# Maxout with two up passes on weight differences, and the first product folded into the down projection

## The chip, the cores and the metric

One core of a Trainium2 chip. The metric is the device time of one execution in microseconds (us), the median of several runs. An execution is also recorded by the hardware profiler; its own time is given beside the span from its first to its last instruction.

## The reference

Attention with exponential features over 8 batches and 8 heads, 576 tokens of 64 elements each, and a maxout feed-forward over the 4608 tokens that come out of it:

```
def phi(x):
    proj = np.einsum('bhsd,df->bhsf', x, w_phi)
    proj = proj - np.max(np.abs(proj), axis=-1, keepdims=True)
    return np.concatenate([np.exp(proj), np.exp(-proj)], axis=-1)
q_p, k_p = (phi(q), phi(k))
kv = np.einsum('bhsf,bhsd->bhfd', k_p, v)
z = np.sum(k_p, axis=2)
num = np.einsum('bhsf,bhfd->bhsd', q_p, kv)
den = np.einsum('bhsf,bhf->bhs', q_p, z)[..., None] + 1e-06
x = (num / den), heads side by side: 4608 x 512
h = np.maximum(np.maximum(x @ w1, x @ w2), x @ w3)     # w1, w2, w3: 512 x 768
return h @ w_out                                       # w_out: 768 x 512
```

## The kernel before

Products are in bf16 with fp32 accumulation in eight PSUM banks. The attention runs in 16 units of four heads (two units make a batch); the feed-forward in nine chunks of 512 tokens: chunk b takes the first 512 tokens of batch b and needs units 2b and 2b+1, chunk 8 takes the last 64 tokens of every batch and needs them all.

A unit's steps, with the names of the profile. q and k are loaded in bf16 (`qk_bf`; units 0 to 3 through GpSimd's DMA queue, which casts on the way, unit 0 in halves; their short tails and all later units come in fp32 through SP's queue as `q_raw`, `k_raw` and are cast by an engine). They are transposed (`tps` to `qkT` by TensorE for units 0 to 3, by DMA later), projected (`psq`, `psk`, `psg`), the maxima taken by VectorE (`mqp`, `mk`), the exponentials by ScalarE (`Ek`, and `Eq` from a second product `psm`). v is multiplied by the scale `em` (`vab`, `vtl`), k's features times v give `kvps` and `kv_sb`, q's features times that give `psn`, VectorE divides (`x_sb`), and TensorE or a DMA transposes into `xT` (`pxT`), the tokens that the feed-forward reads.

A chunk before the change: for each of the three weights and each of six blocks of 128 columns of the hidden layer, four products of 512 columns into `ups`. The first weight's result is copied to `hT` (by ScalarE or VectorE), the second and the third are taken in by VectorE with a maximum (three passes, L757, L763, L765). Then for each of four tiles of 128 tokens six products into `ops` (L784), an eviction to `osb` (L795) and a store. Until the first chunk can start, TensorE is kept busy with products that nothing reads (`warm`).

The weights are loaded once, through GpSimd's queue, with q and k of the first units around them in the order of a string (`ORDER`; in it w0 is w1 of the reference, w1 is w2, w2 is w3, and w3 is w_out).

All steps are nodes of a planner, which runs when the kernel is built. It simulates engines and queues with a cost in microseconds for every node, picks at each moment the ready node with the lowest rank (tables `RANKS` by group of units, `LAGS`, `EVAC` for the feed-forward), chooses the engine where there are several, and so fixes the order of instructions on each engine. On the chip every engine goes through its own order, and waits where an operand or a buffer isn't ready.

Of the kernel before, what the change touches and what calls it, by code (L numbers as in the profile page):

```python
# [10 lines left out]
EXP = mybir.ActivationFunctionType.Exp  # L11
ALU = mybir.AluOpType
# [4 lines left out]
DM = H * D  # L17
DFF = 768
# [17 lines left out]
ORDER = "q0 k0 q1 k1 w0 q2 k2 w1 w2 w3 q3 k3"  # L36
# [6 lines left out]
OSB = 4  # L43
LEAD = 99
# [92 lines left out]
]  # L137
LAGS = [7.954, 12, 11.152, 10.425, 9.54, 8.084, 9.876, -8.613, -11.269]
EVAC = -17.068
FFN = {"up": 0, "down": 0, "t1": 1, "t2": 1, "h": 1, "osb": 1, "store": 1}  # L140


def rank(n):

    if n.kind in FFN:
        return 2 * n.u + LAGS[n.u] + n.at / 11.0 + FFN[n.kind] * EVAC
    if n.kind in ("const", "phi"):
        return -99.0
# [12 lines left out]
class Queues:  # L161
# [4 lines left out]
    UNEVEN = 1.5  # L166
# [11 lines left out]
    def issue(self, n, eng, t, cost):  # L178

        pipes, mine = self.pipes, "POOL" if eng == "POOL" else "SP"  # L180
        other = "SP" if mine == "POOL" else "POOL"
        if n.hold is not None:
            cost = max(cost, pipes[mine] + n.hold - t)
            if n.hold > 0:
                cost = max(cost, pipes[other] + n.hold - t)
        done = t + cost
        end = done
        if n.pipe:
            at = max(done, pipes[mine])
            both = max(0.0, pipes[other] - at)  # L190
            end = at + n.pipe
            if both:
                turns = self.packet[other] / n.packet
                pipes[other] += min(n.pipe, both / turns)
                end += min(both, n.pipe * turns)
            pipes[mine] = end
            self.packet[mine] = n.packet
            if both:
                end += self.UNEVEN
        end += n.lat  # L200
        if not n.pipe and max(pipes.values()) > done:
            end += self.BEHIND
        self.ends[mine] += [end] * n.dmas
        return done, end
# [85 lines left out]
def kernel(  # L290
# [146 lines left out]
    def attention(u):  # L437
# [13 lines left out]
        for what in range(3):  # L451
            raw = raw_bufs(u)[what]
            if what < 2 and by_pe:
                for i, (t0, t1) in enumerate(((0, 8), (8, MT)) if u < HALVES else ((0, MT),)):
                    def main(what=what, t0=t0, t1=t1):
# [281 lines left out]
    def chunk(c_i, ready, tokens_of, out_rows, n_out):  # L737
# [11 lines left out]

        before = [None] * JT  # L750
        for i in range(3):
            for j in range(JT):
                ups = bank("ups", [P, SM])

                def up(i=i, j=j, ups=ups):
                    for ct in range(CT):
                        nc.tensor.matmul(ups(), lhsT=w_bf[i][:, ct, j * P:(j + 1) * P], rhs=tokens_of(ct),  # L757
                                         start=(ct == 0), stop=(ct == CT - 1))
                a = ff("up", {"PE": 0.87}, up, ready + [w_nodes[i]], [ups], pe=True)

                def ev(n_, i=i, j=j, ups=ups):
                    if i == 0:
                        copy_on[n_.eng](hT()[:, j, :], ups())  # L763
                    else:
                        nc.vector.tensor_tensor(hT()[:, j, :], hT()[:, j, :], ups(), ALU.max)  # L765
                e = ff(("t1", "t2", "h")[i], {"ACT": 0.5, "DVE": 0.61} if i == 0 else {"DVE": 0.64}, None,
# [3 lines left out]
                if i == 2:  # L770
                    evac.append(e)
        steps.append(pes)
        for tt in range(SM // P):
# [4 lines left out]
            for i in range(halves):  # L778
# [3 lines left out]
                def down(j0, j1, tt=tt, ops_=ops_, cols=cols, width=width):  # L782
                    for j in range(j0, j1):
                        nc.tensor.matmul(ops_()[:, 0:width], lhsT=hT()[:, j, tt * P:(tt + 1) * P], rhs=wout_bf[:, j, cols],  # L784
                                         start=(j == 0), stop=(j == JT - 1))
                if tt == 0:
                    ff("down", {"PE": 0.87}, lambda f=down: f(0, 4), evac[0:4] + [w_nodes[3]], [hT, ops_], pe=True)
                    count[0] -= 1
                j0 = 4 if tt == 0 else 0
                a = ff("down", {"PE": 1.30 / halves * (JT - j0) / JT}, lambda f=down, j0=j0: f(j0, JT), evac + [w_nodes[3]],  # L790
                       [hT, ops_], pe=True)
# [22 lines left out]
    def weights():  # L814
# [4 lines left out]
        for name in ORDER.split():  # L819
            chain += converted[name] if name != "k0" else []  # L820
            if name == "q0" and HALVES:
# [6 lines left out]
    weights()  # L828
    for b in range(B):
        rows = out[b * S:b * S + SM, :].rearrange("(p j) n -> p j n", j=SM // P)  # L830
        chunk(b, units[2 * b]["done"] + units[2 * b + 1]["done"], lambda ct, b=b: xT[:, b, ct, 0:SM],
              lambda tt, rows=rows: [(rows[:, tt, :], slice(0, P))], 1)
    chunk(B, units[UNITS - 1]["done"], lambda ct: xT[:, :, ct, SM:SM + ST],
# [43 lines left out]
```

## Time and profile before

| | |
|---|---|
| median of 3 runs | 322.58 us (322.11 to 323.34) |
| the profiled execution | 323.14 us, span 321.4 us |
| TensorE busy | 303.3 us, 94% |
| VectorE busy | 235.2 us, 73% |
| ScalarE busy | 209.7 us, 65% |
| GpSimd busy | 117.3 us, 36% |
| mean granted TensorE clock | 0.985 |

In the profile TensorE is PE (its loading of stationary operands PEld), VectorE DVE, ScalarE ACT, GpSimd POOL and SyncE SP. A line of a group of instructions gives source line, engine, operation, output and inputs, the count, busy time in us, mean ns of one, and the idle time of the engine before them with what ended it.

### The profile page before, as it was taken

Reading aid. Unit: us, or ns where it says so; the run is one execution under the profiler, and the core shown is the slowest. Engines: PE = TensorE matmul, PEld = TensorE weight load, DVE = VectorE, ACT = ScalarE, POOL = GpSimd, SP = SyncE. Lnnn points to the kernel's source line nnn. Section 1 sums busy time; section 2 is a strip of 40 time slices with the busy share of each in tenths; the row PEclk is TensorE's granted clock in tenths of the full one; section 3 lists DMA queues with packets and bytes.
Section 4 is the critical chain, followed back from the end, with each engine's and each line's share of the span. In section 5 each row is a group of like instructions: output and inputs, shape, how many; then the busy total and the mean of one; then the engine's idle time right before and its main releaser. Section 6 shows DMA issues by size and latency. Waiting matters only on the chain.

```text
span 321.4 us, 7835 instructions
## 1 busy us (share of the span) xinstructions
PE 303.3 (94%) x3088; PEld 170.3 (53%) x3124; DVE 235.2 (73%) x485; ACT 209.7 (65%) x491; POOL 117.3 (36%) x137
## 2 busy tenths in 40 slices
PE   8999599998999999899999999999999999999993
PEld 3466475556555645644645564546545574444442
DVE  4898973975977995988988878976796686081360
ACT  1597885466979897898698796657707961503301
POOL 8633133170486089083561902635006500000000
PEclk9999899999999999899999999999999999999998
DMA  7999999139868797968997599929803013203005
GB/s 121 224 197 228 233 261 242 44 100 228 232 154 203 245 259 156 255 152 157 200 282 196 84 203 253 245 96 194 140 0 134 1 37 81 98 0 112 21 1 131
DMA packets 87882, 49.79 MB, mean 155 GB/s; under 512 B 56101, under 2 KB 83365, under 8 KB 87845
## 3 DMA queue, kind: packets, MB, share of 16 engines
q1 hardware_dynamic: 81140, 43.98, 56.4%
q0 software_dynamic: 6624, 5.24, 10.4%
q8 instruction: 24, 0.39, 0.5%
q10 hardware_dynamic: 80, 0.07, 0.1%
q14 instruction: 14, 0.11, 0.1%
HBM read 34.67 MB, written 9.44 MB: 137 GB/s over the span
## 4 chain that ended last, share of the span: by engine, by line
PE 74%; DVE 11%; issue 5%; ACT 4%; DMA 2%; POOL 2%; DVEq 0%; POOLq 0%
PE ups L757 42%; PE ops L784 12%; PE kvps L677 6%; PE psn L697 4%; DVE mqp L571 3%; ACT Eq L661 3%; PE psq L558 3%; PE psm L649 3%; DVE x_sb L704 3%; DMA qk_bf<-in_k_dram 2%; DVE mk L571 2%; PE warm L424 1%; PE tps L515 1%; ACT Ek L564 1%; DVE osb L795 1%
## 5 line engine op out<-in xcount | busy, mean ns | idle before, releaser
L757 PE MATMUL ups<-xT,w_bf 128*128 128x512 bf16 x620 | 146.3, 379 | 3.2 <-ACT Eq L661 0.8
L765 DVE TENSOR_TENSOR hT<-hT,ups 128x512 bf16<-128x512 bf16 x108 | 72.7, 685 | 38.8 <-PE ups L757 37.9
L757 PEld LDWEIGHTS <-w_bf 128*128 128x128 bf16 x648 | 61.2, 98 | 71.5 <-issue 3.0
L564 ACT ACTIVATE Ek<-psk 128x512 bf16<-128x512 f32 x128 | 69.7, 621 | 25.6 <-PE psk L558 24.2
L661 ACT ACTIVATE Eq<-psm 128x512 bf16<-128x512 f32 (+1 forms) x160 | 75.4, 591 | 12.3 <-PE psm L649 8.7
L614 POOL TENSOR_TENSOR vab<-v_raw,em 128x1024 bf16<-128x1024 f32 (+1 forms) x30 | 54.2, 1821 | 15.8 <-ACT em L609 15.7
L784 PE MATMUL ops<-wout_bf,hT 128*128 128x512 bf16 (+1 forms) x214 | 49.2, 373 | 0.4
L571 DVE TENSOR_REDUCE mqp<-psq 128x4 bf16<-128x512 f32 x64 | 42.9, 683 | 3.8 <-PE psk L558 3.7
L795 ACT COPY osb<-ops 128x512 f32<-128x512 f32 (+1 forms) x25 | 14.5, 578 | 46.4 <-PE ops L784 46.3
L571 DVE TENSOR_REDUCE mk<-psk 128x4 f32<-128x512 f32 x64 | 42.7, 683 | 0.0
L624 POOL CAST vab<-em 128x32 bf16<-128x32 f32 (+1 forms) x12 | 3.8, 316 | 88.8 <-issue 52.6
L763 ACT CAST hT<-ups 128x512 bf16<-128x512 f32 x47 | 27.6, 590 | 10.6 <-PE ups L757 9.9
L704 DVE TENSOR_TENSOR x_sb<-psn,rden 128x320 bf16<-128x320 f32 x64 | 31.5, 492 | 2.2
L784 PEld LDWEIGHTS <-hT 128*128 128x128 bf16 x222 | 20.9, 98 | 22.0 <-DVE hT L765 0.6
L629 POOL TENSOR_TENSOR vtl<-v_raw,em 64x256 bf16<-64x256 f32 x32 | 20.3, 635 | 21.8 <-ACT em L609 20.6
L697 PE MATMUL psn<-kv_sb,Eq 128*128 128x65 bf16 x640 | 24.8, 195 | 2.1 <-DVE mqp L571 1.2
L697 PEld LDWEIGHTS <-Eq 128*128 128x128 bf16 x640 | 23.1, 98 | 5.9 <-issue 1.7
L677 PEld LDWEIGHTS <-Ek 128*128 128x128 bf16 x640 | 23.7, 101 | 4.5 <-ACT vtl L638 1.2
L677 PE MATMUL kvps<-vab,Ek 128*128 128x65 bf16 x512 | 24.3, 198 | 0.3 <-DVE vab L614 0.2
L677 PE MATMUL kvps<-vtl,Ek 128*128 128x65 bf16 x128 | 21.8, 197 | 1.1 <-ACT vtl L638 1.1
L558 PE MATMUL psk<-w,qkT 64*128 64x128 bf16 x256 | 21.0, 217 | 1.2 <-ACT Eq L661 0.8
L558 PEld LDWEIGHTS <-qkT 64*128 64x128 bf16 x512 | 14.6, 94 | 13.4 <-issue 10.6
(61 smaller groups left out, 267.5 us busy)
## 6 DMA issues: line engine op xcount, KB each, us to landing
v_raw<-in_v_dram SPq DMA_DIRECT2D x16, 512.0 KB, 5.8
out_dram<-osb SPq DMA_DIRECT2D x32, 256.0 KB, 2.5
q_raw<-in_q_dram SPq DMA_DIRECT2D x12, 512.0 KB, 5.7
k_raw<-in_k_dram SPq DMA_DIRECT2D x12, 512.0 KB, 6.2
w_bf<-in_moe_w_dram POOLq DMA_DIRECT2D x3, 768.0 KB, 21.5
q_raw<-in_q_dram SPq DMA_DIRECT2D x16, 64.0 KB, 3.8
k_raw<-in_k_dram SPq DMA_DIRECT2D x16, 64.0 KB, 5.9
v_raw<-in_v_dram SPq DMA_DIRECT2D x16, 64.0 KB, 4.4
```

Source lines behind the costliest of these rows:

```text
L558: nc.tensor.matmul(ps[c]()[:, i, :], lhsT=cols[r, :], rhs=w2[r, c, :], start=True, stop=True)
L564: nc.scalar.activation(Ek[s]()[:, t0:t0 + n, :], ps() if n > 2 else ps()[:, :, 1, :], EXP, scale=1.0 - 2.0 * s)
L571: nc.vector.tensor_reduce((mq, mk)[c]()[:, t0:t0 + n], ps() if n > 2 else ps()[:, :, c, :], AXX, ALU.max, apply_absolute_value=True)
L614: (nc.vector if n_.eng == "DVE" else nc.gpsimd).tensor_tensor(vab()[:, g, t0:t1, 0:D], raw_part(u, 2, t0, t1), em()[:, g, t0:t1].unsqueeze ...
L661: nc.scalar.activation(Eqb()[s][:, cols], psm()[:, 0:n * P], EXP, scale=1.0 - 2.0 * s)
L677: nc.tensor.matmul(kvps()[:, ab, g, :], lhsT=Ek[g]()[:, t, :], rhs=vab()[:, g, t, :] if c < 4 else vt()[:, g, pr, ab, :], start=(c == 0), ...
L697: nc.tensor.matmul(psn()[:, c, :], lhsT=Eqb()[g][:, t0:t0 + P], rhs=kv()[:, pr, ab, g, :], start=(g == 0), stop=(g == 1))
L704: nc.vector.tensor_tensor(x_sb()[:, pr, :, ab, :], psn()[:, :, 0:D], rden().to_broadcast([P, 5, D]), ALU.mult)
L757: nc.tensor.matmul(ups(), lhsT=w_bf[i][:, ct, j * P:(j + 1) * P], rhs=tokens_of(ct), start=(ct == 0), stop=(ct == CT - 1))
L763: copy_on[n_.eng](hT()[:, j, :], ups())
L765: nc.vector.tensor_tensor(hT()[:, j, :], hT()[:, j, :], ups(), ALU.max)
L784: nc.tensor.matmul(ops_()[:, 0:width], lhsT=hT()[:, j, tt * P:(tt + 1) * P], rhs=wout_bf[:, j, cols], start=(j == 0), stop=(j == JT - 1))
```

## The change

It rests on max(a, b, c) = a + max(0, b - a, c - a). With a = x w1 the up projection needs products with w2 - w1 and w3 - w1 only, and a's share of the output, x (w1 w_out), is added in the accumulation of the down projection. So:

- VectorE subtracts w1 from w2 and from w3 in place, in bf16, each in two halves of 128 x 1536 (`wd`).
- TensorE transposes w1 (24 transposes, `pwT`), the result is copied to a buffer of `hT`, and multiplied with w_out: four times six products into `pm`. The copies of `pm` (`line_w`) overwrite the first 512 columns of w1.
- A chunk has two up passes. The first is evicted with a maximum with zero, the second with VectorE's maximum as before. Each down tile begins with four products of the tokens with `line_w`, and goes on with the six of `hT` with w_out.
- Eight copies on GpSimd put the last 64 tokens of each batch side by side for the last chunk (into the other columns of w1 and into `x_last`).
- k of unit 0 comes through SP's queue in fp32 (`K0_SP`), with a cast on VectorE or ScalarE.
- The order of loads, `RANKS`, `LAGS`, `EVAC`, the step of the feed-forward's ranks and the planner's rule for two queues at once get other values. So the whole order of instructions is new.

```diff
-ORDER = "q0 k0 q1 k1 w0 q2 k2 w1 w2 w3 q3 k3"
+ORDER = "q0 k0 q1 k1 w0 q2 k2 w3 w1 q3 k3 w2"
...
+K0_SP = 1
...
-LAGS = [7.954, 12, 11.152, 10.425, 9.54, 8.084, 9.876, -8.613, -11.269]
-EVAC = -17.068
-FFN = {"up": 0, "down": 0, "t1": 1, "t2": 1, "h": 1, "osb": 1, "store": 1}
+LAGS = [11.676, 11.801, 9.456, 10.469, 7.828, 8.2, 10.732, 10.134, 2.767]
+EVAC = -53.283
+FFN = {"up": 0, "down": 0, "t1": 1, "h": 1, "osb": 1, "store": 1, "wd": 1, "wt": 0, "we": 1, "wm": 0, "mo": 1}
+STEPS = 8.5
...
-        return 2 * n.u + LAGS[n.u] + n.at / 11.0 + FFN[n.kind] * EVAC
+        return 2 * n.u + LAGS[n.u] + n.at / STEPS + FFN[n.kind] * EVAC
...
-            if both:
+            if both and done > self.CALM:
                 end += self.UNEVEN
...
+    line_w = w_bf[0][:, :, 0:DM]
+    x_last = [w_bf[0][:, :, DM:DFF], const.tile([P, CT, DFF - DM], BF16, name="x_last")]
...
+                    if u == 0 and what == 1 and K0_SP:
+                        def main(t0=t0, t1=t1):
+                            nc.sync.dma_start(raw_part(0, 1, t0, t1).rearrange("p (h j) d -> p h (j d)", j=SM // P),
+                                              k[0, t0 // 4:t1 // 4, 0:SM, :].rearrange("h (p j) d -> p h (j d)", p=P))
...
-        for i in range(3):
+        for i in range(2):
             for j in range(JT):
...
-                        nc.tensor.matmul(ups(), lhsT=w_bf[i][:, ct, j * P:(j + 1) * P], rhs=tokens_of(ct),
+                        nc.tensor.matmul(ups(), lhsT=w_bf[i + 1][:, ct, j * P:(j + 1) * P], rhs=tokens_of(ct),
...
-                a = ff("up", {"PE": 0.87}, up, ready + [w_nodes[i]], [ups], pe=True)
+                a = ff("up", {"PE": 0.87}, up, ready + diffs[i], [ups], pe=True)
...
-                    if i == 0:
-                        copy_on[n_.eng](hT()[:, j, :], ups())
+                    if i == 1:
+                        nc.vector.tensor_tensor(hT()[:, j, :], hT()[:, j, :], ups(), ALU.max)
+                    elif n_.eng == "ACT":
+                        nc.scalar.activation(hT()[:, j, :], ups(), RELU)
                     else:
-                        nc.vector.tensor_tensor(hT()[:, j, :], hT()[:, j, :], ups(), ALU.max)
+                        nc.vector.tensor_scalar_max(hT()[:, j, :], ups(), 0.0)
...
+                def straight(tt=tt, ops_=ops_, cols=cols, width=width):
+                    for ct in range(CT):
+                        nc.tensor.matmul(ops_()[:, 0:width], lhsT=tile_of(ct, tt), rhs=line_w[:, ct, cols],
+                                         start=(ct == 0), stop=False)
...
-                                         start=(j == 0), stop=(j == JT - 1))
-                if tt == 0:
-                    ff("down", {"PE": 0.87}, lambda f=down: f(0, 4), evac[0:4] + [w_nodes[3]], [hT, ops_], pe=True)
...
+                                         start=False, stop=(j == JT - 1))
+                ff("down", {"PE": 0.87 / halves}, straight, ready + lines, [ops_], pe=True)
+                count[0] -= 1
+                a = ff("down", {"PE": 1.30 / halves}, down, evac + [w_nodes[3]], [hT, ops_], pe=True)
...
+    for i in range(2):
+        for h in range(2):
+            def diff(n_, i=i, h=h):
+                dst, c = w_bf[i + 1], slice(2 * h, 2 * h + 2)
+                (nc.vector if n_.eng == "DVE" else nc.gpsimd).tensor_tensor(dst[:, c, :], dst[:, c, :], w_bf[0][:, c, :],
+                                                                           ALU.subtract)
...
+                    nc.tensor.transpose(pwT()[:, i, ct, :], w_bf[0][:, ct, (2 * g + i) * P:(2 * g + i + 1) * P], ident)
...
+                nc.tensor.matmul(pm(), lhsT=w1T()[:, j, ct * P:(ct + 1) * P], rhs=wout_bf[:, j, :],
+                                 start=(j == 0), stop=(j == JT - 1))
+        n_ = wnode("wm", {"PE": 1.30}, mult, turned + diffs[0] + diffs[1] + [w_nodes[3]], [pm, w1T], at=8)
...
+        lasts.append(node("C", 2 * b + 1, {"POOL": 0.4}, lambda b=b: nc.gpsimd.tensor_copy(
+            x_last[b // 4][:, :, b % 4 * ST:(b % 4 + 1) * ST], xT[:, b, :, SM:SM + ST]),
```

More of the change, by code (lines that the diff above doesn't have):

```diff
@@ L11 @@
 EXP = mybir.ActivationFunctionType.Exp
+RELU = mybir.ActivationFunctionType.Relu
 ALU = mybir.AluOpType
@@ L43 @@
 OSB = 4
+K0_SP = 1
+BY_POOL = ()
 LEAD = 99
@@ L165 @@
     BEHIND = 2.5
-    UNEVEN = 1.5
+    UNEVEN, CALM = 1.5, 6.0
     def __init__(self):
@@ L454, in attention, with to_bf16 @@
                 for i, (t0, t1) in enumerate(((0, 8), (8, MT)) if u < HALVES else ((0, MT),)):
+                    if u == 0 and what == 1 and K0_SP:
+                        def main(t0=t0, t1=t1):
+                            nc.sync.dma_start(raw_part(0, 1, t0, t1).rearrange("p (h j) d -> p h (j d)", j=SM // P),
+                                              k[0, t0 // 4:t1 // 4, 0:SM, :].rearrange("h (p j) d -> p h (j d)", p=P))
+                        n_ = nd("L0" if i == 0 else "const", {"SP": 0.62}, main, [], [raw], pipe=0.133 * (t1 - t0), lat=1.7,
+                                at=what, packet=59.0)
+                        def to_bf16(n_, t0=t0, t1=t1):
+                            copy_on[n_.eng](qk()[:, 1, t0:t1, :], raw_part(0, 1, t0, t1))
+                        n_ = nd("C", {"DVE": 0.42, "ACT": 0.55}, None, [n_], [raw, qk])
+                        n_.fn = lambda n_=n_, f=to_bf16: f(n_)
+                        cast[1, i] = cast[1, 1] = n_
+                        continue
                     def main(what=what, t0=t0, t1=t1):
@@ L735, with chunk @@
     last_ff, steps = [None], []
-    def chunk(c_i, ready, tokens_of, out_rows, n_out):
+    def chunk(c_i, ready, tokens_of, tile_of, out_rows, n_out):
         hT = buf("hT", 2, [P, JT, SM], BF16)
@@ L769, in chunk @@
                 before[j] = e
-                if i == 2:
+                if i == 1:
                     evac.append(e)
@@ L780, in chunk, with down @@
                 cols = slice(i * width, (i + 1) * width)
-                def down(j0, j1, tt=tt, ops_=ops_, cols=cols, width=width):
-                    for j in range(j0, j1):
-                        nc.tensor.matmul(ops_()[:, 0:width], lhsT=hT()[:, j, tt * P:(tt + 1) * P], rhs=wout_bf[:, j, cols],
-                                         start=(j == 0), stop=(j == JT - 1))
-                if tt == 0:
-                    ff("down", {"PE": 0.87}, lambda f=down: f(0, 4), evac[0:4] + [w_nodes[3]], [hT, ops_], pe=True)
[L788 to L791, printed above, removed]
+                def straight(tt=tt, ops_=ops_, cols=cols, width=width):
+                    for ct in range(CT):
+                        nc.tensor.matmul(ops_()[:, 0:width], lhsT=tile_of(ct, tt), rhs=line_w[:, ct, cols],
+                                         start=(ct == 0), stop=False)
+                def down(tt=tt, ops_=ops_, cols=cols, width=width):
+                    for j in range(JT):
+                        nc.tensor.matmul(ops_()[:, 0:width], lhsT=hT()[:, j, tt * P:(tt + 1) * P], rhs=wout_bf[:, j, cols],
+                                         start=False, stop=(j == JT - 1))
+                ff("down", {"PE": 0.87 / halves}, straight, ready + lines, [ops_], pe=True)
+                count[0] -= 1
+                a = ff("down", {"PE": 1.30 / halves}, down, evac + [w_nodes[3]], [hT, ops_], pe=True)
                 part = osb or buf("osb", OSB, [P, DM], FP32)
@@ L819, in weights @@
         for name in ORDER.split():
-            chain += converted[name] if name != "k0" else []
-            if name == "q0" and HALVES:
+            if name == "k0" and HALVES:
+                continue
+            chain += converted[name]
+            if name == "q0" and HALVES and not K0_SP:
                 chain[-2:] = [converted["q0"][0], converted["k0"][0], converted["q0"][1], converted["k0"][1]]
@@ L828, with wnode, turn, turned_out @@
     weights()
+    diffs, lines, turned = [[], []], [], []
+    def wnode(*args, at):
+        return node(args[0], 0, *args[1:], at=at)
+    for i in range(2):
[4 more added lines that the diff above has]
+                                                                           ALU.subtract)
+            n_ = wnode("wd", {"DVE": 0.87}, None, [w_nodes[0], w_nodes[i + 1]], [], at=6 * i - 2)
+            n_.fn = lambda n_=n_, f=diff: f(n_)
+            diffs[i].append(n_)
+    w1T = buf("hT", 2, [P, JT, SM], BF16)
+    for g in range(JT // 2):
+        pwT = bank("pwT", [P, 2, CT, P], BF16)
+        def turn(g=g, pwT=pwT):
+            for i in range(2):
+                for ct in range(CT):
+                    nc.tensor.transpose(pwT()[:, i, ct, :], w_bf[0][:, ct, (2 * g + i) * P:(2 * g + i + 1) * P], ident)
+        def turned_out(n_, g=g, pwT=pwT):
+            copy_on[n_.eng](w1T()[:, 2 * g:2 * g + 2, :].rearrange("p i n -> p (i n)"),
+                            pwT().rearrange("p i c n -> p (i c n)"))
+        n_ = wnode("wt", {"PE": 0.6}, turn, [w_nodes[0], n_ident], [pwT], at=4)
+        n_t = node("we", 0, {"ACT": 0.95, "DVE": 1.15}, None, [n_], [pwT, w1T], locks=[pwT], at=4)
+        n_t.fn = lambda n_=n_t, f=turned_out: f(n_)
+        turned.append(n_t)
+    for ct in range(CT):
+        pm = bank("pm", [P, DM])
+        def mult(ct=ct, pm=pm):
+            for j in range(JT):
+                nc.tensor.matmul(pm(), lhsT=w1T()[:, j, ct * P:(ct + 1) * P], rhs=wout_bf[:, j, :],
+                                 start=(j == 0), stop=(j == JT - 1))
+        n_ = wnode("wm", {"PE": 1.30}, mult, turned + diffs[0] + diffs[1] + [w_nodes[3]], [pm, w1T], at=8)
+        n_t = node("mo", 0, {"ACT": 0.5, "DVE": 0.61}, None, [n_], [pm], locks=[pm], at=8)
+        n_t.fn = lambda n_=n_t, ct=ct, pm=pm: copy_on[n_.eng](line_w[:, ct, :], pm())
+        lines.append(n_t)
     for b in range(B):
@@ L831 @@
         chunk(b, units[2 * b]["done"] + units[2 * b + 1]["done"], lambda ct, b=b: xT[:, b, ct, 0:SM],
+              lambda ct, tt, b=b: xT[:, b, ct, tt * P:(tt + 1) * P],
               lambda tt, rows=rows: [(rows[:, tt, :], slice(0, P))], 1)
-    chunk(B, units[UNITS - 1]["done"], lambda ct: xT[:, :, ct, SM:SM + ST],
+    lasts = []
+    for b in range(B):
+        lasts.append(node("C", 2 * b + 1, {"POOL": 0.4}, lambda b=b: nc.gpsimd.tensor_copy(
+            x_last[b // 4][:, :, b % 4 * ST:(b % 4 + 1) * ST], xT[:, b, :, SM:SM + ST]),
+            units[2 * b]["done"] + units[2 * b + 1]["done"] + diffs[0] + diffs[1] + turned, []))
+    chunk(B, lasts, lambda ct: xT[:, :, ct, SM:SM + ST],
+          lambda ct, tt: x_last[tt // 2][:, ct, tt % 2 * P:(tt % 2 + 1) * P],
           lambda tt: [(out[(2 * tt + i) * S + SM:(2 * tt + i + 1) * S, :], slice(i * ST, (i + 1) * ST))
```

2 lines of the change are left out of this document (1 added, 1 removed), and 66 rows, old and new, of the table RANKS.

## The prediction

> **What bounds the kernel now.** I read the page's first part, then busy time by stretch, with the stretches cut at three events: the first up product (46.73), the end of the last attention product (265.30) and the end of the last product of all (316.30).
>
> ```profile
> span 321.4 us, 7835 instructions
> PE 303.3 (94%) x3088; PEld 170.3 (53%) x3124; DVE 235.2 (73%) x485; ACT 209.7 (65%) x491; POOL 117.3 (36%) x137
> ```
>
> ```profile
> core 0: us, PE busy (x) PEld busy (x) DVE busy (x) ACT busy (x) POOL busy (x), PEclk, DMA share, GB/s
> 0.00:46.73 46.73, 41.40 (x567) 26.42 (x568) 38.33 (x92) 32.51 (x81) 22.95 (x39) 0.96 1.12 212
> 46.73:265.30 218.57, 211.19 (x2289) 120.44 (x2319) 175.02 (x359) 163.31 (x388) 94.30 (x98) 0.99 0.70 166
> 265.30:316.30 51.00, 50.74 (x238) 23.47 (x240) 21.41 (x37) 13.87 (x24) 0.00 (x0) 1.00 0.19 57
> 316.30:321.40 5.10, 0.00 (x0) 0.00 (x0) 0.42 (x1) 0.00 (x0) 0.00 (x0) 0.69 0.54 122
> ```
>
> From 46.73 to 316.30, that is 269.57 us, TensorE is the limit: it stands still for 7.38 us in the middle stretch and 0.26 us in the one after, 7.64 in all, while VectorE has 43.6 us free and ScalarE 55.3 in the middle one. Before 46.73 TensorE only looks busy (warm products fill it); there the loads and VectorE set the pace. The last 5.10 us are an eviction and a store, which the change leaves alone.
>
> TensorE's real rates are read from runs of one kind in the chain of waits in order of time (start, length, what), because a single product's duration overlaps the next one.
>
> ```profile
> 4.65 6.64 DMA qk_bf<-in_k_dram
> 11.34 0.63 PE tps L515 x15
> 51.21 1.01 PE tps L515 x32
> 74.51 1.28 PE kvps L677 x40
> 80.06 0.45 PE pxT L718 x5
> 269.57 5.18 PE ops L784 x24
> 295.47 15.54 PE ups L757 x72
> ```
>
> 72 products of 512 columns in 15.54 us and 24 in 5.18 both give 0.216 us each. A transpose takes 0.032 to 0.09 us.
>
> **The change, part by part.**
>
> *TensorE after the first up product.* The three up passes become two: 9 chunks x 6 column blocks x 4 = 216 products go, 216 x 0.216 = -46.6 us. In the down projection each of 36 tiles gets 4 products with w1 w_out, the last of them split into two half-width ones: worth 144, +31.1. Making w1 w_out takes 24 products (`pm`), +5.2. In the built order of instructions, unit 2's 40 kvps products now come behind the first up product (+1.3, the row of 40) and unit 3's 32 tps transposes come ahead of it (-1.0). Sum: **-10.0 us**, so 269.57 becomes 259.6 if TensorE stands still as long as before.
>
> *Does it?* VectorE and ScalarE must keep up with a shorter stretch.
>
> ```profile
> L765 DVE TENSOR_TENSOR hT<-hT,ups 128x512 bf16<-128x512 bf16 x108 | 72.7, 685 | 38.8 <-PE ups L757 37.9
> L763 ACT CAST hT<-ups 128x512 bf16<-128x512 f32 x47 | 27.6, 590 | 10.6 <-PE ups L757 9.9
> L763 DVE CAST hT<-ups 128x512 bf16<-128x512 f32 x7 | 4.8, 688 | 2.0 <-PE ups L757 1.9
> L614 DVE TENSOR_TENSOR vab<-v_raw,em 128x512 bf16<-128x512 f32 x5 | 4.7, 979 | 0.0
> L518 DVE COPY qkT<-tps 128x1024 bf16<-128x1024 bf16 x8 | 5.3, 685 | 8.3 <-PE tps L515 8.3
> L682 DVE CAST kv_sb<-kvps 128x260 bf16<-128x260 f32 x18 | 7.6, 426 | 6.7 <-PE kvps L677 6.7
> L721 DVE COPY xT<-pxT 128x576 bf16<-128x576 bf16 x7 | 3.1, 452 | 0.7 <-PE pxT L718 0.7
> L721 ACT COPY xT<-pxT 128x576 bf16<-128x576 bf16 x5 | 3.4, 673 | 0.2 <-PE pxT L718 0.2
> L502 DVE CAST qk_bf<-q_raw 128x128 bf16<-128x128 f32 x2 | 0.5, 280 | 0.0
> ```
>
> 54 of 108 maxima leave VectorE; in the middle stretch 79 become 42 by the built order (37 x 0.685 = -25.3). The first evictions, now with a maximum with zero, stand 16 on VectorE and 38 on ScalarE in the built order (7 and 47 before). I price that maximum like the cast that it replaces, 0.69 and 0.59; it reads the same bank and writes the same tile. VectorE so gets +9 x 0.69 = +6.2, ScalarE -5.3. The built order shifts more: six output evictions of 0.69 go from VectorE to ScalarE (-4.1, +3.5 at 0.59), each gets two copies of `pm` (+1.4, +1.2), VectorE two `vab` multiplies (some +2.2) and the second difference (+2.8, below), ScalarE nine copies of xT and of `vab`, at most 0.67 each (+6.0). VectorE comes to 158 us and ScalarE to 169. The stretch would be 259.6 less the 212 products that stand behind the last attention product, 213.8: 74% and 79%, against 80% and 75% now. The most loaded helper does not get busier, so I keep the 7.64 us of idle. The waits of TensorE in that stretch are many small ones:
>
> ```profile
> PE psn L697 <- DVE mqp L571: 1.2, 2, 0.8
> PE pxT L718 <- DVE x_sb L704: 0.8, 1, 0.8
> PE ups L757 <- DVE hT L765: 0.6, 1, 0.6
> ```
>
> The bounds are 4 us less (VectorE lighter) and 7 more, if the idle doubles because all orders are new. The eight copies into `x_last` and `w0_bf` on GpSimd cost nothing: they are needed by the last chunk alone, and GpSimd has 124 us free in the middle stretch; without that cover, one would delay a `vab` by less than a microsecond.
>
> *The start.* k's first halves leave GpSimd's DMA queue for SP's, in fp32, with a cast on VectorE. The chain above waits until 11.29 for k's second half, the fourth transfer in GpSimd's queue. What is late next is q's second half, third in that queue and second after the change:
>
> ```profile
> 3.40 0.72 POOL L457 DMA_DIRECT2D qk_bf<-in_q_dram  x1
> ...
> qk_bf<-in_q_dram POOLq DMA_DIRECT2D x1, 128.0 KB, 4.9
> ```
>
> 3.40 + 4.9 = 8.3: a gain of 3.0 us, between nothing (if VectorE sets the start anyhow) and the whole 6.64. Against it stands VectorE, busy for 38.33 of 46.73 us and this close to full after the wait:
>
> ```profile
> 11.34:46.73 35.39, 31.67 (x505) 22.32 (x506) 31.97 (x68) 28.48 (x73) 13.47 (x21) 0.95 1.21 233
> ```
>
> By the built order, what it does ahead of the first up eviction loses four tail casts (-1.1), three `kv_sb` casts (-1.3) and two xT copies (-0.9), and gains one `vab` half (+1.0), one copy of the turned w1 (+0.7, the 1024-column copy), two casts of k and two halves of w2 - w1. The trace has no 512-column fp32 cast from SBUF: between the 0.28 of 128 columns and the 0.98 of the multiply; I take 0.5. Nor has it a subtraction of 1536 columns with all in bf16: from 0.9, if two columns go at a time, to 2.9, at the multiply's 0.979 per 512; I take 1.4, since the multiply reads fp32. Net +2.2 us, from +0.9 to +6.2. The start moves to 46.73 - 3.0 + 2.2 = **45.9**. The Trainium skill, in "VectorE: DVE Perf Modes", section "What auto-detection actually checks", says that a two-tensor operation with all operands 16-bit reaches the doubled mode and no more; worked out from its 0.96 GHz that would be an estimated 0.8 us each and a time of 310.6; no row here shows such an operation.
>
> *The transposes of w1.* 24 of them stand in TensorE's order ahead of unit 0's and 1's psm products, so these wait for w1 to land. By the row of 32 tps they take 0.8 us, by that of 5 pxT 2.2; they lie where warm products now run, and I count nothing.
>
> **The sum.** 45.9 + 259.6 + 5.1 = 310.6 us of span. The profiled execution took 323.14 us with a span of 321.4, the median of the runs is 322.58, so 1.2 us above that span: **311.8 us**.
>
> **The rivals.**
>
> *The middle stretch keeps its length.* The helpers nearly fill their densest part:
>
> ```profile
> 100.00:120.00 20.00, 19.29 (x256) 11.74 (x258) 18.70 (x43) 18.50 (x43) 8.27 (x10) 1.00 0.91 243
> ```
>
> If the attention work, and not TensorE, sets the 218.57 us, only the end shrinks: behind the last attention product the built order has 212 products instead of 238, 26 x 0.216 = 5.6, and the start gives 0.8. That is 322.6 - 6.4 = 316 us, and with ScalarE's 4 us more on the path 320. For it: ScalarE's added copies. Against it: 43.6 and 55.3 us free over the whole stretch. Chance 0.17.
>
> *Slower: w3 holds up the first chunk.* The second difference, and w1 w_out behind it (it overwrites w1), now need a weight that comes last in GpSimd's queue, behind q and k of unit 3.
>
> ```profile
> L430 POOL DMA_DIRECT2D w_bf<-in_moe_w_dram x3: 770/792/800, 6.9 to 9.8; - x3
> ...
> DMA to landing us min/median/max: 14.8/21.5/25.4
> ```
>
> ```profile
> 19.57 0.81 POOL L457 DMA_DIRECT2D qk_bf<-in_k_dram  x1
> ...
> qk_bf<-in_k_dram POOLq DMA_DIRECT2D x1, 256.0 KB, 28.0
> ```
>
> Now w3 lands at 9.8 + 25.4 = 35.2 and the last transfer of that queue, k of unit 3, at 47.6. The same transfers less two halves of k put w3 at about 46 to 48. The subtraction stands in VectorE's order with unit 3's reductions queued behind it; on TensorE the seventh up block waits for it, and all that is queued behind. TensorE gets there some 8 us after the start (24 up products 5.2, 40 kvps 1.3, unit 3's projections), at about 54, and VectorE needs 1.8 to 5.8 us for both halves: no loss up to a landing at 48 to 52, and after it each microsecond is lost whole. Slower than before begins at 10.8 us of loss, a landing at about 61. With a landing at 65, as if the loads for units 4 and 5 on SP's queue went first, the time is about 327. Against it: 47.6 is 13 us from there. Chance 0.08.
>
> *TensorE's saving isn't there* since the 4 + 6 products of a down tile run slower than the 0.216 of the ops row: it would take 0.244 for each of the 360 to eat 10 us, giving 322. Nothing speaks for it; chance 0.02.
>
> *The transposes go one by one*, without overlap, and hold up psm:
>
> ```profile
> L718 PE MATMUL pxT<-ident,x_sb 128*128 128x128 bf16 x60 | 5.2, 220 | 1.0 <-DVE x_sb L704 0.8
> ```
>
> 24 x 0.220 = 5.3 us against the 0.8 to 2.2 above: a start some 4 us later, 316 us. Against it stand the two runs of the chain, 32 in 1.01 and 5 in 0.45. Chance 0.03. The Trainium skill, "TensorE: Matmul & The Clock Gate", Part 4, gives about 275 ns for a transpose in a kernel's context, which one by one would be an estimated 6.6 us; the trace disagrees, with 32 in 1.01 us.
>
> **How the numbers follow.** The forecast has the rest, 0.70: its own bounds are a start from 42 to 50 (-3.9, +4.1) and idle of -4 to +7, hardly all at once, so 306 to 318. The range reaches into the first rival, 306 to 320, and leaves out some 0.2. What a measurement of this kernel can tell from no change is about 0.5%, or 1.6 us: faster means below 321.0. The forecast gives 0.69 of faster and 0.01 of same, the transposes 0.03 of faster, the first rival 0.14, 0.02 and 0.01 of slower, the w3 rival 0.01 of same and 0.07 of slower, the slow products 0.01 of same and of slower: 0.86, 0.05, 0.09.
>
> **What would show it.** Right: two `ups` passes and ten products per `ops` tile at 0.216 us; the first up product at 44 to 48; TensorE busy at the same share behind it, its idle there near 8 us; maxima on VectorE 54 instead of 108. Wrong: a wait of ups for the subtraction or for w_bf of several microseconds near 50; kvps, psn or psq waiting for VectorE or ScalarE for more than 15 us in all; the first up product after 50, with w1's transposes waiting for w1's load while psm queues behind.

## The result and the profile after

The changed kernel takes **309.38 us** (median of 4 runs, 309.02 to 311.62) where the one before takes 322.55: a ratio of 0.960, 95% interval 0.956 to 0.965. The forecast was 311.8, in a range from 306 to 320.

Of the profile after: the page's span and first line of busy time, then busy time by stretch, cut at the same three events as before (the first up product, the end of the last attention product, the end of the last product), and from the page the chain's shares by engine.

```profile
span 307.2 us, 7766 instructions
...
PE 293.9 (96%) x3070; PEld 167.4 (54%) x3106; DVE 212.9 (69%) x444; ACT 213.2 (69%) x495; POOL 118.6 (39%) x139
...
PE 92%; DVE 3%; ACT 2%; issue 1%; DVEq 0%
```

```profile
core 0: us, PE busy (x) PEld busy (x) DVE busy (x) ACT busy (x) POOL busy (x), PEclk, DMA share, GB/s
0.00:46.86 46.86, 42.63 (x584) 27.61 (x586) 41.01 (x90) 33.77 (x82) 23.89 (x40) 0.96 1.13 218
46.86:257.50 210.64, 205.71 (x2271) 118.23 (x2302) 161.54 (x338) 165.47 (x390) 94.28 (x98) 0.99 0.70 171
257.50:303.40 45.90, 45.59 (x219) 21.55 (x220) 9.89 (x18) 13.98 (x24) 0.40 (x1) 1.00 0.26 73
303.40:307.20 3.80, 0.00 (x0) 0.00 (x0) 0.42 (x1) 0.00 (x0) 0.00 (x0) 0.89 0.50 112
```

The 14.2 us between the two spans divide so: the start +0.1 (46.73 to 46.86), the middle stretch -7.9 (218.57 to 210.64), the stretch of the last chunks -5.1 (51.00 to 45.90), and what follows the last product -1.3 (5.10 to 3.80; a store's landing, which no experiment looked at). Behind the first up product TensorE is busy for 251.30 us, 261.93 before, which is 10.6 less, and stands still for 5.2 us, 7.64 before. Its share of the chain of waits went up from this line of the page before:

```profile
PE 74%; DVE 11%; issue 5%; ACT 4%; DMA 2%; POOL 2%; DVEq 0%; POOLq 0%
```

The pieces of the change, in groups by line and shape, and the subtraction's row from the view of the tile `w_bf` (min/median/max in ns, first and last start):

```profile
L786 DVE TENSOR_TENSOR hT<-hT,ups 128x512 bf16<-128x512 bf16 x54 | 36.6, 684 | 40.4 <-PE ups L780 38.5 <-ACT Eq L683 1.5
L788 ACT ACTIVATE hT<-ups 128x512 bf16<-128x512 f32 x38 | 23.0, 605 | 9.2 <-PE ups L780 9.0
L790 DVE TENSOR_SCALAR hT<-ups 128x512 bf16<-128x512 f32 x16 | 11.0, 690 | 8.1 <-PE ups L780 8.1
L883 ACT COPY hT<-pwT 128x1024 bf16<-128x1024 bf16 x2 | 1.9, 1035 | 0.0
L883 DVE COPY hT<-pwT 128x1024 bf16<-128x1024 bf16 x1 | 0.7, 673 | 0.0
L471 DVE CAST qk_bf<-k_raw 128x512 bf16<-128x512 f32 x2 | 1.0, 508 | 0.4 <-DMA k_raw<-in_k_dram 0.4
...
L868 DVE TENSOR_TENSOR w_bf<-w_bf x4: 945/947/950, 37.7 to 50.0; 128x1536 bf16<-128x1536 bf16 x4
```

The sizes are near those of the forecast: 54 maxima, the maximum with zero at 0.605 and 0.690 us, k's cast 0.508. Only the subtraction is faster, 0.947 us where I took 1.4.

### The profile page after: what moved, and what is told of

The parts are those of the page before. It is cut to its first block, busy times and chain, and to the rows that moved or that the text cites. A ratio compares the mean times of both kernels' runs of the same rounds, so it can differ in the third digit from the quotient of the medians.

```text
span 307.2 us, 7766 instructions
## 1 busy us (share of the span) xinstructions
PE 293.9 (96%) x3070; PEld 167.4 (54%) x3106; DVE 212.9 (69%) x444; ACT 213.2 (69%) x495; POOL 118.6 (39%) x139
## 4 chain that ended last, share of the span: by engine, by line
PE 92%; DVE 3%; ACT 2%; issue 1%; DVEq 0%
PE ups L780 30%; PE ops L814 15%; PE ops L809 10%; PE kvps L699 7%; PE psn L719 7%; PE warm L431 6%; PE psq L580 5%; PE psm L671 4%; PE pm L894 2%; PE tps L537 1%; PE psm L675 1%; DVE mqp L593 1%; ACT Ek L586 1%; PE psm L673 1%; PE psg L575 1%; PE pxT L740 1%
## 5 line engine op out<-in xcount | busy, mean ns | idle before, releaser
L780 PE MATMUL ups<-xT,w_bf 128*128 128x512 bf16 x414 | 98.3, 379 | 1.2 <-DVE mqp L593 0.2
L780 PEld LDWEIGHTS <-w_bf 128*128 128x128 bf16 x432 | 40.7, 98 | 45.5 <-issue 0.5
L786 DVE TENSOR_TENSOR hT<-hT,ups 128x512 bf16<-128x512 bf16 x54 | 36.6, 684 | 40.4 <-PE ups L780 38.5
L636 POOL TENSOR_TENSOR vab<-v_raw,em 128x1024 bf16<-128x1024 f32 (+1 forms) x27 | 49.8, 1858 | 25.2 <-ACT em L631 24.5
L814 PE MATMUL ops<-wout_bf,hT 128*128 128x512 bf16 (+1 forms) x216 | 51.6, 374 | 0.4 <-issue 0.2
L822 ACT COPY osb<-ops 128x512 f32<-128x512 f32 (+1 forms) x31 | 18.0, 580 | 44.5 <-PE ops L814 43.3
L809 PE MATMUL ops<-w_bf,xT 128*128 128x512 bf16 x121 | 32.6, 380 | 0.5
L788 ACT ACTIVATE hT<-ups 128x512 bf16<-128x512 f32 x38 | 23.0, 605 | 9.2 <-PE ups L780 9.0
L580 PE MATMUL psq<-w,qkT 64*128 64x128 bf16 x256 | 22.8, 218 | 0.6 <-DVE mqp L593 0.5
L699 PE MATMUL kvps<-vab,Ek 128*128 128x65 bf16 x512 | 22.7, 194 | 0.0
```

The source lines that it names most:

```text
L580: nc.tensor.matmul(ps[c]()[:, i, :], lhsT=cols[r, :], rhs=w2[r, c, :], start=True, stop=True)
L636: (nc.vector if n_.eng == "DVE" else nc.gpsimd).tensor_tensor(vab()[:, g, t0:t1, 0:D], raw_part(u, 2, t0, t1), em()[:, g, t0:t1].unsqueeze ...
L699: nc.tensor.matmul(kvps()[:, ab, g, :], lhsT=Ek[g]()[:, t, :], rhs=vab()[:, g, t, :] if c < 4 else vt()[:, g, pr, ab, :], start=(c == 0), ...
L780: nc.tensor.matmul(ups(), lhsT=w_bf[i + 1][:, ct, j * P:(j + 1) * P], rhs=tokens_of(ct), start=(ct == 0), stop=(ct == CT - 1))
L809: nc.tensor.matmul(ops_()[:, 0:width], lhsT=tile_of(ct, tt), rhs=line_w[:, ct, cols], start=(ct == 0), stop=False)
```

## The experiments

Theory: the time follows the number of TensorE's products behind the first up product. Rivals: VectorE's relief paid; the newly searched order paid; the attention work keeps the middle stretch at its length. Ratios are to the kernel before, run on the same chip in between, with 95% intervals.

**The new algebra in the old order.** `RANKS`, `LAGS`, `EVAC`, `STEPS`, `ORDER`, `K0_SP` and the queue rule as before.

```diff
-ORDER = "q0 k0 q1 k1 w0 q2 k2 w3 w1 q3 k3 w2"
+ORDER = "q0 k0 q1 k1 w0 q2 k2 w1 w2 w3 q3 k3"
...
-K0_SP = 1
+K0_SP = 0
...
-EVAC = -53.283
+EVAC = -17.068
...
```

> The new algebra with the order of loads, the rank tables, LAGS, EVAC and k's way of the kernel before. Theory (TensorE's products set the time, 10.0 us fewer): most of the gain of 13.2 us stays, 311 to 317 us, the rest being the order's. Rival (the newly searched order brought the gain, the algebra little): 319 us or more.

Measured: 330.19 us, ratio 1.024 (1.021 to 1.028). That is the rival's side, and beyond it: the algebra alone, with the old tables, not only gains little but loses 7.4 us (322.84 before, in the same series). Its busy time in two stretches, cut at the first up product and at the end of the last product:

```profile
core 0: us, PE busy (x) PEld busy (x) DVE busy (x) ACT busy (x) POOL busy (x), PEclk, DMA share, GB/s
0.00:62.20 62.20, 53.52 (x720) 33.90 (x723) 50.86 (x107) 43.24 (x101) 28.94 (x44) 0.95 1.02 200
62.20:324.70 262.50, 248.27 (x2353) 136.77 (x2381) 162.26 (x337) 170.08 (x396) 90.34 (x94) 0.98 0.57 141
```

The first up product comes 15.5 us later than before, and behind it 7.1 us are saved. That is little: all 24 products `pm` stand ahead of the first up product here (the last starts at 53.7), so by the prediction's sum 15 us should have gone behind it. TensorE stands still there for 14.2 us. In its chain of waits unit 1's tokens are late, behind GpSimd's `vab`, and behind products `pm` that no chunk needs yet:

```profile
41.23 2.61 POOL vab L636
43.84 1.56 POOL vtl L651
45.47 0.97 POOL vtl L651
46.48 1.59 PE kvps L699 x26
48.06 1.87 PE pm L894 x5
```

**The old algebra in the new order.** Chunk function of before, tables, loads and k's way of after (`STEPS` 11, since a chunk has more steps).

```diff
-STEPS = 8.5
+STEPS = 11.0
...
-        for i in range(2):
+        for i in range(3):
             for j in range(JT):
...
```

> The old algebra (three up passes, six products in a down tile) with the order of loads, k's way, rank tables, LAGS and EVAC of the changed kernel. Rival (the newly searched order alone is faster): 318 us or less. Theory (the algebra's fewer products, which need an order of their own): no faster than before, 321 us or more.

Measured: 331.70 us, ratio 1.028 (1.024 to 1.032). The new tables by themselves are no gain; the rival falls in its simple form. These tables were fitted to other steps, though, and no run has the old algebra with tables searched anew, so what a longer search alone could have brought stays open. The trace sets it a bound: behind the first up product TensorE is busy for 261.93 us in the kernel before, which is more than the whole 256.54 us of that stretch after the change. An order that leaves these products there could not have reached it.

**The new algebra with the old tables, but the new loads and k's new way.** `STEPS` and the queue rule stay new, too.

```diff
-LAGS = [11.676, 11.801, 9.456, 10.469, 7.828, 8.2, 10.732, 10.134, 2.767]
-EVAC = -53.283
+LAGS = [7.954, 12, 11.152, 10.425, 9.54, 8.084, 9.876, -8.613, -11.269]
+EVAC = -17.068
... (and RANKS of before)
```

> The new algebra with the rank tables, LAGS and EVAC of before, but the new order of loads and k's new way. In the run with everything old, the first up product came at 62.2 instead of 46.9 and the time was 330. If the loads did that: the first up product below 52 and 312 to 319 us. If the tables did: still near 60 and 325 us or more.

Measured: 336.54 us, ratio 1.044 (1.038 to 1.049), and each expectation half right. The first up product is at 48.1, so these loads go with an early start; the time is lost behind it, where the middle stretch takes 241.6 us with TensorE, VectorE and ScalarE further from full (the cut lies 1 us behind the last attention product). TensorE stands still for 18.5 us of it; its granted clock is 0.96, in the changed kernel's middle stretch 0.99, so a part of the loss is slower products:

```profile
48.10:289.70 241.60, 223.15 (x2337) 125.97 (x2335) 158.09 (x328) 170.32 (x405) 95.77 (x99) 0.96 0.60 152
```

**Fewer products in the changed kernel.** In its own order, without the products with w1 w_out.

```diff
-                    for ct in range(CT):
-                        nc.tensor.matmul(ops_()[:, 0:width], lhsT=tile_of(ct, tt), rhs=line_w[:, ct, cols],
-                                         start=(ct == 0), stop=False)
+                    ops_()
...
-                                         start=False, stop=(j == JT - 1))
+                                         start=(j == 0), stop=(j == JT - 1))
```

> The changed kernel in its own order, without the products of the tokens with w1 w_out (worth 144 of 512 columns; they are left out of the output). Theory (TensorE is the limit wherever they stand): 144 x 0.216 = 31 us less, 278 us, or up to 283 if the helpers then begin to bind. Rival (attention work on VectorE and ScalarE sets the middle stretch): only the part behind the attention shrinks, some 7 to 12 us, 297 to 302 us.

Measured: 294.13 us, ratio 0.912 (0.909 to 0.916): 15.3 us less, half of 31, between theory and rival. The two stretches, cut at the end of the last attention product:

```profile
48.10:249.10 201.00, 186.65 (x2174) 109.01 (x2201) 158.91 (x333) 164.47 (x390) 94.48 (x98) 1.00 0.76 177
249.10:286.50 37.40, 36.24 (x171) 16.71 (x172) 10.64 (x20) 13.99 (x24) 0.40 (x1) 1.00 0.31 86
```

Behind the attention the products count nearly whole: 44 go there, 9.5 us by the price of 0.216, and 8.5 come off, since TensorE now stands still for 1.2 us in that stretch. In the middle 100 go, worth 21.6, and 9.6 come off; TensorE now stands still for 14.4 us there, in many small waits, at a granted clock of 1.00. VectorE's share of the chain rises to this:

```profile
PE 69%; DVE 17%; ACT 8%; issue 3%; DMA 2%; DVEq 0%
```

**More products in the changed kernel.** The same four products twice.

```diff
-                    for ct in range(CT):
+                    for n, ct in enumerate(list(range(CT)) * 2):
                         nc.tensor.matmul(ops_()[:, 0:width], lhsT=tile_of(ct, tt), rhs=line_w[:, ct, cols],
-                                         start=(ct == 0), stop=False)
+                                         start=(n == 0), stop=False)
```

> The changed kernel in its own order, with the four products of a down tile with w1 w_out done twice (worth 144 more products of 512 columns; the first term counts double in the output). Leaving them out gained 15 of 31 us. If TensorE is the limit wherever they stand, adding them costs the whole 31 us: 340 us. If waits for VectorE and ScalarE hide some: 325 to 335 us.

Measured: 341.68 us, ratio 1.059 (1.057 to 1.062): 32.3 us more, the whole price, 0.224 per product. In the middle nothing hides them, and TensorE is as full as it was (this cut lies 1 us behind the last attention product):

```profile
47.40:281.90 234.50, 231.01 (x2408) 129.25 (x2406) 163.44 (x338) 165.90 (x390) 94.51 (x98) 0.99 0.64 154
```

So the changed kernel stands at a balance. On average a product added costs 0.22 us, and one taken away in the same order gains 0.11.

**VectorE's work given back to the changed kernel.** Every maximum of the second pass twice, in its own order.

```diff
                         nc.vector.tensor_tensor(hT()[:, j, :], hT()[:, j, :], ups(), ALU.max)
+                        nc.vector.tensor_tensor(hT()[:, j, :], hT()[:, j, :], ups(), ALU.max)
```

> The changed kernel in its own order, with each of the 54 maxima of the second pass done twice: VectorE gets back the 37 us of work that the change took from it, TensorE's products stay. Theory (products): at most +4 us, 309 to 313 us. Rival (it was VectorE's relief that paid): the gain goes, 318 us or more.

Measured: 335.17 us, ratio 1.038 (1.036 to 1.041): 25.8 us more for 37 us of VectorE. The theory had at most 4, and fails. A block of 128 hidden columns has four products, 0.864 us, and now 1.37 us of maxima, so VectorE sets the second pass even in the last chunks (50.20 us of stretch, 45.90 without). In the middle it adds 21.8:

```profile
48.00:280.40 232.40, 213.68 (x2271) 119.92 (x2301) 185.61 (x373) 166.60 (x390) 94.32 (x98) 0.99 0.62 154
280.40:330.60 50.20, 46.29 (x219) 21.28 (x220) 18.88 (x35) 13.98 (x24) 0.40 (x1) 1.00 0.24 69
```

This puts the double load in one pass, where the kernel before had it spread over two; it shows that VectorE's 37 us could not have stayed in this order, not what they cost before.

**The kernel before without the second pass's maxima.** In its own order; the products stay.

```diff
-                    else:
+                    elif i == 2:
                         nc.vector.tensor_tensor(hT()[:, j, :], hT()[:, j, :], ups(), ALU.max)
```

> The kernel before in its own order, where the second pass's products are made but not taken in: the 54 maxima that the change takes from VectorE go, and TensorE's products stay. Theory: 0 to 3 us less (the idle of TensorE that waits for VectorE), 319.5 to 322.5 us. Rival (VectorE's relief paid): 8 us less or more, under 315 us.

Measured: 322.24 us, ratio 0.998 (0.996 to 0.999): about 0.7 us. VectorE's relief by itself paid next to nothing.

**The kernel before with a quarter of the third pass's products.**

```diff
-                    for ct in range(CT):
+                    for ct in range(CT if i < 2 else 1):
...
-                                         start=(ct == 0), stop=(ct == CT - 1))
+                                         start=(ct == 0), stop=(ct == CT - 1 or i == 2))
```

> The kernel before in its own order, where each block of the third up pass does one of its four products (162 products of 512 columns are left out; all evictions stay). Theory (TensorE is the limit before, too): 162 x 0.216 = 35 us less, 288 us, up to 293 with some new waits. Rival (VectorE and ScalarE set the middle stretch): under 15 us less, 308 us or more.

Measured: 316.92 us, ratio 0.982 (0.979 to 0.985): 6.0 us of 35. That decides nothing: the third pass kept its maxima, 0.685 us for each block of one product of 0.216, so VectorE set its pace, and of the 46.7 us of that pass at most 9.7 could go. TensorE waits for it at 22 down tiles, and its granted clock was 0.97, against 0.99 before:

```profile
PE ops L784 <- DVE hT L765: 7.6, 22, 1.4
```

**The kernel before without its third pass, products and maxima,** so that VectorE's part goes, too.

```diff
+                    ups()
-                    for ct in range(CT):
+                    for ct in range(CT if i < 2 else 0):
...
-                    else:
+                    elif i == 1:
```

> The kernel before in its own order, with the third up pass left out whole: 216 products (46.6 us of TensorE) and 54 maxima (37 us of VectorE); w3 takes no part in the output. If TensorE's products count whole: 276 us. If the attention work sets a floor under the middle stretch, as leaving out the products with w1 w_out from the changed kernel showed (31 us of products, 15 us of time): 290 to 300 us. This is the work of that kernel (294.1 us) in the old order: near 294, the two orders are equally good for it; well above, the new order fits the helpers better.

Measured: 297.68 us, ratio 0.922 (0.919 to 0.925): 24.9 us for 46.6 us of products and 37 of maxima. It is 0.115 us per product, near the 0.106 in the changed kernel. The middle stretch shrinks by 11.8 (218.57 to 206.80), the last chunks by 14.1, cut at the first down product behind the attention. The granted clock counts here: 0.96 in the middle stretch, 0.99 before, so a part of the missing gain is slower products. The time is 3.6 us above the 294.1 of the new order, with less work than there (no subtractions, no `pm`). The new order fits it a little better; how much of the 3.6 us is the order and how much the clock, no run tells.

```profile
47.20:254.00 206.80, 186.86 (x2172) 110.79 (x2168) 152.20 (x324) 162.82 (x388) 94.39 (x98) 0.96 0.75 175
254.00:290.90 36.90, 36.74 (x174) 16.89 (x174) 9.45 (x17) 13.86 (x24) 0.00 (x0) 1.00 0.26 79
```

**k of unit 0 through GpSimd's queue** in the changed kernel's own order.

```diff
-                            nc.sync.dma_start(raw_part(0, 1, t0, t1).rearrange("p (h j) d -> p h (j d)", j=SM // P),
+                            nc.gpsimd.dma_start(qk()[:, 1, t0:t1, :].rearrange("p (h j) d -> p h (j d)", j=SM // P),
...
-                            copy_on[n_.eng](qk()[:, 1, t0:t1, :], raw_part(0, 1, t0, t1))
+                            pass
```

> The changed kernel in its own order, with k of unit 0 through GpSimd's queue, cast on the way, and without VectorE's two casts. By the prediction's term the first products come up to 3 us later and the first up product goes from 46.9 to about 49: 311 to 312 us. By what the trace of the changed kernel suggests (ScalarE and VectorE set the start, whose up product came no sooner than before) the time stays within 1 us of 309.4.

Measured: 313.57 us, ratio 0.974 (0.968 to 0.979); the first up product at 49.0, 2.1 later. The time is 4.2 us above the changed kernel's and above both expectations. Between the two profiles it is 3.6 us, 1.5 of them behind the first up product, and no run tells what made those. The prediction's term stands for the start, and what I read from the trace after (that k's way no longer mattered) was wrong.

**Without the making of w1 w_out,** and **without the subtractions,** each in the changed kernel's own order.

```diff
-                for ct in range(CT):
+                for ct in range(0):
                     nc.tensor.transpose(pwT()[:, i, ct, :], ...
...
-            for j in range(JT):
+            for j in range(0):
                 nc.tensor.matmul(pm(), ...
```

> The changed kernel in its own order, without the making of w1 w_out: no transposes of w1, no products pm and none of their copies; the first 512 columns of w1 stand in its place, so the output lacks the right first term. Theory: 24 products less, 5.2 us, and a start up to 2 us sooner since ScalarE loses two copies of the turned w1 there: 302 to 304.5 us. Rival (they lie beside other work): 308 us or more.

Measured: 308.63 us, ratio 0.956 (0.953 to 0.959), not clear of the changed kernel's. The first up product comes at 45.0, 1.9 sooner, and the middle stretch is no shorter:

```profile
45.00:256.30 211.30, 203.66 (x2248) 118.06 (x2278) 160.12 (x336) 164.22 (x388) 94.44 (x98) 0.98 0.70 173
```

So 5.2 us of products gained nothing there. TensorE is busy for only 2.0 us less than in the changed kernel and stands still for 2.7 us more, 2.0 of them where kvps waits for `vab`. After that wait products run slower: the 40 psn products behind it take 2.39 us, in the changed kernel 1.42, and from 60 to 80 us the granted clock is 0.91, there 1.00.

```diff
-                (nc.vector if n_.eng == "DVE" else nc.gpsimd).tensor_tensor(dst[:, c, :], dst[:, c, :], w_bf[0][:, c, :],
-                                                                           ALU.subtract)
+                pass
```

> The changed kernel in its own order, without the four subtractions (the up products then use w2 and w3 themselves, and the output is another). If VectorE sets the start, its two subtractions of 0.95 us ahead of the first up product come off: 307.5 to 308 us. If ScalarE's chain sets it, nothing: 309 to 309.7 us.

Measured: 309.58 us, ratio 0.959 (0.956 to 0.962), the first up product at 47.3: VectorE's subtractions lie on nothing that sets the time.

## Why the prediction was right, point by point

**TensorE's sum, -10.0.** The stretch from the first up product to the last product went from 269.57 to 256.54, -13.0. Of that, 10.6 are TensorE's busy time (261.93 to 251.30) and 2.4 its idle (7.64 to 5.2). So the sum of products was right, `pm` included, and the 3.1 us by which the stretch beat the forecast are mostly idle that I had kept. What the prediction lacked is the condition. I counted each product as 0.216 us of time. The runs show that price for added products (0.224) and about half of it for those taken away in a fixed order (0.106 and 0.115): when TensorE gets shorter, waits for the attention work of the other engines take much of the gain.

The weak step is "269.57 becomes 259.6 if TensorE stands still as long as before". I had kept the idle because the most loaded helper does not get busier, and that is no ground for it: with the old tables VectorE and ScalarE are less full in the middle stretch (65% and 70%, with the new loads), and TensorE stands still for 18.5 us. The new algebra lost 7.4 us with everything old and 14.0 with the old tables alone. What the change has besides the algebra is an order fitted to it, in which the chain is 92% TensorE's instead of 74%. Neither half of the change gained by itself in these runs. I had priced the order only as a chance for idle, and it could have decided the sign; that the idle stayed small was in this sense lucky. How the tables reach the fit, by which rank, no run here tells.

**The middle stretch's helpers.** VectorE 77% and ScalarE 79%, forecast 74 and 79; idle 5.2, forecast 7.64 with bounds of -4 and +7. The rival that the middle stretch keeps its length did not come, but something like its floor shows when far more products go: the stretch stays at 201 and 207 us in two kernels. Both are fixed orders made for more products, so whether another order would go below is not shown.

**The 24 products `pm`, +5.2.** They are in TensorE's busy time as forecast, but leaving them out shortened nothing behind the first up product. In a fixed order that tells only what can be taken from it, not what they had cost.

**The start, 45.9 against 46.86.** The first up product moves by itself: three runs whose edits touch nothing ahead of it have it at 47.4, 48.0 and 48.1. From 40 to 46 us the granted clock is 0.72 in the changed kernel's profile and 0.50 in the later two. So the shifts below are good to about a microsecond. k's way was worth 2.1 us at the first up product, forecast 3.0. VectorE's net of +2.2 (its lower end adds up to +0.8, not +0.9) was the wrong engine: the subtractions, two of which I had put there at 1.4, cost nothing. What I left out was ScalarE with its two copies of the turned w1, 1.035 us each, and the transposes themselves. The chain runs through the transposes, though through `warm` products on both sides of them, and later through ScalarE:

```profile
20.73 1.47 PE pwT L880 x24
...
38.74 0.49 ACT Eq L683
```

Transposes and copies together were worth 1.9 us; the runs don't part them. The transposes took 0.061 us each, so that rival (one by one, at 0.220) fell. The Trainium skill, "TensorE: Matmul & The Clock Gate", Part 4, has about 275 ns for a transpose in a kernel's context. The trace has a duration of 219 ns for one, below that, and in a row of 24 a new one every 61 ns: the page's figure is to be compared with the first, not, as I did, with the second.

**The subtraction.** 0.947 us for 1536 columns fits the doubled mode, and my 1.4 from the fp32 multiply was too high. The Trainium skill, "VectorE: DVE Perf Modes", "Side-by-side: where the cycles go", adds a fixed part of about 158 cycles to the doubled reads: (768 + 158) / 0.96 GHz gives an estimated 0.965 us. The trace agrees; the 0.8 that I had worked out from the mode alone was short of it.

**w3 last.** Its row of issue and its time to landing, from the timeline of GpSimd and from the DMA issues of that window:

```profile
16.46 0.77 POOL L437 DMA_DIRECT2D w_bf<-in_moe_w_dram  x1
...
w_bf<-in_moe_w_dram POOLq DMA_DIRECT2D x1, 768.0 KB, 28.1
```

It lands at 44.6, forecast 46 to 48, and the subtraction that needs it starts at 49.2 without a wait for it. That rival was far off. A late start did come in the old order, but from unit 1's attention, not from a weight.

## What to carry to other kernels

A TensorE that is 94% busy is not a TensorE whose every product costs its time: look at the engines' shares of the chain, and test with products both added and taken away, since the two prices can differ by a factor of two. Where a planner or a search has fitted the order to the work, an edit and its order are one change: price the edit by what the other engines allow, and don't count on the same edit in an old order; here it lost 7 to 14 us. And when a step leaves an engine, list what every engine of that stage gets in its place; here I missed ScalarE's two copies. Read the granted clock beside every comparison: in two of the runs above products also ran slower where TensorE waited more.

## What the runs showed that was not expected

A bf16 copy of 1024 columns from PSUM takes 1.035 us on ScalarE and 0.673 on VectorE (576 columns, before the change: 0.673 and 0.452), while fp32 results of 512 columns leave PSUM faster on ScalarE (0.605 against 0.690, with the maximum with zero): which engine is the cheaper one turned around with the type.

Slower products followed waits of TensorE. Without the making of w1 w_out, two waits of 2.0 us in all stand ahead of products at 1.7 times their time, 40 psn in 2.39 us instead of 1.42. That the wait brings the lower clock is read from the order in time alone. Without the products with w1 w_out, many small waits, 14.4 us in all, left the middle stretch at a granted clock of 1.00.
